# A new hand-written order for a one-core block-sorted attention and feed-forward kernel

## The chip, the cores and the metric

The kernel runs on one core of a Trainium2 chip. A core has five engines that run side by side, each through its own list of instructions: TensorE (PE in the profile; PEld is its weight load), VectorE (DVE), ScalarE (ACT), GpSimd (POOL) and SyncE (SP). They meet through semaphores: an instruction waits until a count is reached, and everything behind it on the same engine waits with it. Transfers between the chip's memory and the core's are issued by GpSimd or SyncE and then run on 16 DMA engines by themselves.

The metric is the device time of one execution in microseconds, the median of several runs. Less is better.

## The reference

Four batches of eight heads, 768 positions, head size 64. A matrix `sort_net` of 8x8 for each head is made doubly stochastic in five rounds (Sinkhorn), and mixes the eight blocks of 96 positions of k and of v. Attention is then local: each block of q sees its mixed block alone. A feed-forward layer with a leaky slope follows.

```python
for _ in range(5):
    P = P - np.max(P, axis=-1, keepdims=True)
    P = np.exp(P)
    P = P / (np.sum(P, axis=-1, keepdims=True) + 1e-09)
    P = P / (np.sum(P, axis=-2, keepdims=True) + 1e-09)
k_sorted = np.einsum('bhij,bhjcd->bhicd', P, k_b).reshape(B, H, S, D)
v_sorted = np.einsum('bhij,bhjcd->bhicd', P, v_b).reshape(B, H, S, D)
...
scores = scale * np.matmul(q_b, k_sb.transpose(0, 1, 2, 4, 3))
attn = softmax(scores)
attn_out = np.matmul(attn, v_sb).reshape(B, H, S, D)
...
x = attn_out.transpose(0, 2, 1, 3).reshape(B * S, H * D)   # 3072 x 512
h = x @ w_in                                               # 512 x 2048
g = np.maximum(h, 0.0) + alpha * np.minimum(h, 0.0)
return g @ w_out                                           # 2048 x 512
```

## The kernel before

The program first records some 1,230 operations with what each reads and writes, and then lays them out on the engines in an order that is written down by hand in two tables.

The work. A unit of attention is a group `g` of 0 to 31: one block of 96 positions of one batch, all eight heads. Groups 0 to 7 are batch 0, and so on. The steps, with the lines that the profile names:

- *Loads.* GpSimd issues the loads: q of batch 0 (L397, into a part of `hT` that is free then), k and v of batch 0 (L419, into `KS0` and `VST0`), k and v of batch 1 (L419 and L435, into `KS1` and `VST1`), `w_in` in four pieces (L907), `w_out` in two (L912), q of batches 1 to 3 in eight pieces each (L401, into `QN`). Later batches reuse the two buffers. In `QN`, `VDz`, `KSz` and `Esb` zeros are written once by GpSimd's memsets (L461, L456, L453, L474); a q piece may come only behind the memset of its own part of `QN`.
- *Sinkhorn.* Five rounds of six small VectorE operations and an exponential on ScalarE (L521); the last writes `Pb`. TensorE spreads it (L539), and VectorE makes the mixing matrix `BDK` of batch 0 (L543). For later batches L557, L560 and L565 to L585 make `BDM` and `BDV`.
- *Queries* of batch 0: six groups of 16 matmuls turn them (L600), ScalarE copies them to `QTz` (L372, the line of every plain copy on ScalarE or VectorE). Of later batches, SyncE turns them by six DMA transposes per batch (L409).
- *Keys* (`prep_k`): six groups per batch. Batch 0 multiplies `KS` by `BDK` (L600). Later batches are first copied into the zero-padded `KSz` (L616, three slots), then multiplied by `BDM` (L629). A copy of each group goes to `KT`. For batch 0 the first two groups are also copied to a pad (L642).
- *Values* (`prep_v`): eight groups per batch: a copy into place (batch 0: L653 into `hT`, later: L658 into `VDz`, four slots), matmuls (L674 or L669), a copy to `VS`.
- *Attention.* Scores (L715 for batch 0, L712 later), a row maximum on VectorE (L721), for batch 0 the scores transposed with the maximum subtracted (L736, L727) and one exponential (L759); later eight exponentials (L748) and a DMA transpose (L753). Then the product with the values (L768), a reciprocal and a scaling (L776, L779, to `xq`), and a transpose into `xT`: matmuls (L794) and a copy for batches 0 and 1, a DMA (L787) later.
- *Feed-forward.* Chunks of tokens: groups 0 and 1, 2 and 3, and from then on four groups at a time. The first layer: for each of 16 slices of `w_in` four matmuls (L823; 192 columns in the first two chunks, 384 later) into one of two banks of `psH` (in the first chunk also a bank of `psYP`), a negated relu on ScalarE (L833, into `t`) and one combining operation on VectorE (L836, into `hT`). The bank is free when L836 has run. The second layer: for each of 24 tiles of 128 tokens four times four matmuls (L862), a copy to `outstg` and a store (L876).
- *Fillers.* L808 are matmuls whose results nobody reads; they only keep TensorE busy.

What sets the order. `SEQ` lists the recorded operations by number; `arrange` walks it and appends each operation to the list of its engine. Operations that more than one engine can do carry a letter (p GpSimd, a ScalarE, d VectorE): the copies of L372, L616, L642, L653 and L658 are such. `WARM` adds fillers: `89:10:y` puts ten in front of operation 89, in bank y. `emit` works out which waits are needed. So the tables decide which engine does a copy and in which order each engine runs, and nothing else. GpSimd's operations other than DMAs run strictly one behind the other.

```python
def arrange(self, table):
    letters = {"p": "pool", "a": "act", "d": "dve"}
    ...
    for n, x in enumerate(table):
        op = self.ops[int(x.rstrip("pad"))]
        e = letters.get(x[-1], op.engs[0])
        assert e in op.engs and op.deps <= done
        done.add(op.idx)
        op.eng, op.pos, op.start = e, len(self.order[e]), float(n)
        self.order[e].append(op)
```

Of the kernel before, what the change touches and what calls it, by code (L numbers as in the profile page):

```python
# [37 lines left out]
12p 61 62 63 132 64 65 31 89 66 32 83 37 13 81 67 84 87 68 91 69 88 85 70 71 10 72 130 73 40 74 90 133 75 76 86 41  # L38
77 131 78 82 79 134 92 80 93 102 26 94d 147 103a 148 104 95 105a 100 98 99a 38 109d 106p 108p 107p 114 35 36 96a
97p 146 110p 250p 248p 113p 30 135 249p 254p 24 144 143 145 253p 20 111d 16 112d 21 141 140 142 313p 347p 139 403  # L40
404 34 33 115d 101a 158 118 116 119a 120 149 124 159 121d 125a 160 136 117d 122 137 150 123d 161 126 128 151 127a
152 129d 17 247d 162 163 164 153 177 154 155 165 166d 156 184 167 157a 196 193 194 197 185 168 169 195 27 198 170
186 187 199 202 205 188 214 203 204 200 201 220 217 215 218 206 207 189 221 219 226 222 227 229 216 190 228 230 223
224 171 231 225 208 273 235 236 237 191 238 192a 232 261 251 209 262 233 252a 239 240 241 210 263 211 255 270 212
256a 234 213d 301d 175 264 291 242 259 271 260a 265 274 267 292 272 243 266 244 279 293 282 245 280 268 281 285 294
286 258p 257p 352p 311p 300p 312p 310p 351p 348p 305p 275 338 269 174 304d 283 246d 302 303a 287 284 295 314 288
339 306 340 315 289 307a 296 316 290 176 297 320 317 276 341 318 321 319 322 178 179 298 379 308 299a 380 309a 323
342 326 349 324 327 350a 381 343 344 325 328 345 353 329 332 382 330 333 346d 354d 383 357 331 335 334 277a 361 373
336 362 358a 384 385 337 363 419 386 364 367 365 368 572p 374 402 360p 574p 391p 355p 359d 420 421 366 388 370 371
356d 387d 389d 369 372 375 392 435 436 429 393a 430 396 376 432 397d 431 377d 573p 395p 577p 390p 398 394p 445p  # L50
578p 446p 447p 449p 437 180 183 182 422 181 438 453 454 433 399d 448p 455 405 465 400 401a 459 434 466 460 461 456
451 452d 406 483 423 477 457 458 462 467 495 407 408 415 475p 413 418 411 412 479p 480p 450d 172 478a 481 506p 509p
414 463 484 424 476d 425 505p 510p 482a 496 464 409d 485 486 487 426 549 427d 488 439 507 497 492 440 508d 441 489
493 511 442 525 494 490 516 491 443a 512a 517 468 378 498 278 526 518 513 514 527 417 535p 571p 416 536p 537 469
550 515 470 471 538d 519 520 522 472 561 523 473a 539 540a 521 562 524 543 544 563 499 541 551 500 501 546 502 542d
575 503a 547 528 428 534 474 564 444 597 545 576d 555 529 606 556 548 558 607a 559 552 530 557 531 560 610 579 553a
570 613d 598 637d 612p 609p 608p 611a 582 580 583 599 581 532 635 591 636d 638p 584 585 586 587 592 639 588 626
533a 640a 589 627 590 614 615 628 641 565 593 617 618 600 566 616 642d 567 620 621 594 677 568 619 623 622 678 595a
569a 624 659 660 601 602 603 625 646 644 643 645 718p 713p 714p 661 662 663 679 604 668 704 671 629 504 410 605a
669 672 705 664 665 630 719 673 670 631 632 674 686 706 633 666a 675 692 739 554 680 752p 687 634a 648 649 748p 650  # L60
720a 676 681 689 716d 688 698 715p 647 749d 717d 658 652 690 691 699 700 173 750 693 778p 753p 854p 777p 751a 701
702 721 694 695 754 722 740 682 703 723 741 724 727 755d 683 696a 725 726 728 707 667 596 742 779 733 768 730 731
780a 729 756 708 734 783 735 757 848d 769 770 732 709 782d 758 762 759 784d 710 763 760 764 761 743 781d 744 812p
654 655 657 813p 651 849p 656 847p 850p 853p 653 814 736 803 785 737d 815a 786 765 766 804 788 789 805 767 787 745
771 711 684 806 697 738 746 794 797 838 816 798 817a 795 839 799 840 772 790 773 796 774 818 791 820 792a 775 793
841 800 801 821 807 819d 851 826 873 802 822 823 852a 824 832 881 833 827 828 874 888p 882a 834 855 885 911p 887p
875 825 808 884d 809 883d 835 856 857 842 829 912p 886a 909 861 836 830a 837 862 858 901 867 910a 843 863 889 859
860 890 902 913 864 865 903 868 869 891 895 844 914d 866 896 897 747 846 685 712 831 876 811 915 892 870 877 904
810 776 917 893 916a 935 894 871a 918 898 920 921 899 936 937 919 900 878 929 926 879 961 927 930 962 928 931 905
906 907 922 981 923 932 963 880 938 845 943 987 933 934 924d 944 964 908 982 939 946 988 989 990 983 949 947 945  # L70
940 955 941 965 950 1007 956 948 958 959 951 952 1008 1009 960 972 957 973 966 967 969 984 1033 974 970 953a 971
978 985a 979 975 976 1034 980 991 992 977 1035 1010 872 925 1036 942 968 954 1018 998 1019 995 1020 999 996 1000
1004 1059 997 1005 993 1060 1001 1002 1021 1047 1011 1061 1003 1006 1015 1016 1024 1025 1017 1012 1026 1048 1022d
1013 1085 1027 1030 1079 1080 1028 1031 1032 1029 1044 1045 1086 1041 1042 1023 1014 994 1062 986 1087 1081 1049
1046 1043 1053 1054 1055 1037 1056 1050 1067 1105 1057 1058 1070 1051d 1038 1116 1117 1068 1071 1039 1072 1069 1076
1077 1106 1078 1073 1063 1082 1074 1075 1064 1096 1083a 1097 1065 1098 1093 1094 1095 1118 1119 1120d 1107 1102
1103 1104 1040 1088 1108 1099 1089 1137 1122 1100 1101 1123 1090 1091 1124 1113 1161 1109 1128 1114 1115 1129 1110
1111 1130 1084 1066 1052 1092 1112 1125 1138 1134 1126 1127 1135 1136 1131 1139 1146 1132 1133 1147 1148 1143 1144
1145 1162 1140 1149 1163 1152 1141a 1150 1151 1155 1182 1183 1153 1154 1156 1157 1167 1168 1169 1158 1221 1184 1173
1159 1160 1174 1175 1170 1209 1179 1171 1172 1180 1181 1176 1222 1185 1191 1177 1178 1188 1189 1192 1190 1203 1210  # L80
1194 1164 1211 1121 1195 1196 1200 1186a 1187 1142 1193 1201 1165d 1202 1197 1198 1199 1204 1205 1206 1207a 1166
1208 1212 1223 1213a 1214 1224 1215 1216 1225 1226 1217 1218 1219 1220
# [947 lines left out]
```

## Time and profile before

| | us |
|---|---|
| median of 3 runs | 239.45 |
| the runs | 238.71, 241.29, 239.45 |
| the profiled execution | 238.55 |
| its span, first to last instruction | 236.8 |
| first L823 (feed-forward) starts | 30.30 |
| last L862 ends | 234.2 |

The span is what the rows of the profile divide up; the profiled execution's own time is 1.75 us longer. Mean granted clock of TensorE over the span: 0.992.

In the rows below a group of instructions reads: line, engine, operation, out<-in, sizes, count; for groups by line then busy us and mean ns of one, and the engine's idle time in front of them with what ended it. In the timeline a row starts with start and length in us, and a bracket gives the idle time in front of the instruction and its releaser.

### The profile page before, as it was taken

The page shows a single profiled execution, that of the slowest core. Times are in us where ns is not written, and L with a number is a line of the kernel's source. Part 1 is how long each engine was busy: PE and PEld are TensorE (multiplying, and loading weights), DVE is VectorE, ACT ScalarE, POOL GpSimd, SP SyncE. Part 2 cuts the span into 40 slices and gives each one's busy share as a digit, 9 for nine tenths or more (in the row PEclk, how much of TensorE's full clock was granted, in tenths as well). Part 3 has the DMA queues.
Part 4 walks back from the last instruction along what each step waited for, and adds up shares of the span by engine and source line. Part 5 has one row for each costly group of instructions (what it writes and reads, how often), then busy time and mean ns, then how long its engine had stood idle before and what let it go on. Part 6 is the DMA issues. An engine that isn't in the chain of part 4 may idle for free.

```text
span 236.8 us, 6180 instructions
## 1 busy us (share of the span) xinstructions
PE 226.7 (96%) x2474; PEld 142.7 (60%) x2503; DVE 169.4 (72%) x353; ACT 151.7 (64%) x423; POOL 73.3 (31%) x140
## 2 busy tenths in 40 slices
PE   7798899999999999999999999999999999999995
PEld 3346688687666666566655665655555555555544
DVE  4737688989899997869897667676766577644240
ACT  4465257587887988886768786756863646353232
POOL 7939824805879221148390020000000000000000
PEclk9999799999999999999999999999999999999999
DMA  5999999999999998999999797652442323400033
GB/s 95 214 214 212 205 219 195 173 212 162 181 92 145 141 168 125 154 182 194 130 100 92 210 157 157 98 95 42 125 106 69 97 50 84 132 3 0 1 136 133
DMA packets 70941, 31.36 MB, mean 132 GB/s; under 512 B 64504, under 2 KB 65280, under 8 KB 70912
## 3 DMA queue, kind: packets, MB, share of 16 engines
q0 software_dynamic: 22384, 13.63, 42.0%
q1 hardware_dynamic: 48528, 17.33, 36.9%
q8 instruction: 20, 0.33, 0.6%
q14 instruction: 9, 0.07, 0.1%
HBM read 27.28 MB, written 6.29 MB: 142 GB/s over the span
## 4 chain that ended last, share of the span: by engine, by line
PE 88%; DMA 5%; POOL 3%; DVE 2%; issue 1%; ACT 1%; POOLq 0%
PE psH L823 34%; PE psYP L862 30%; DMA VST<-in_v_dram 5%; PE psS L862 4%; PE psS L712 4%; PE psO L768 3%; PE psYP L669 2%; PE psYP L629 2%; PE psS L727 2%; PE psO L794 1%; PE psS L736 1%; PE psS L715 1%; POOL VDz L456 1%; POOL hT L653 1%; PE psH L808 1%
## 5 line engine op out<-in xcount | busy, mean ns | idle before, releaser
L836 DVE SCALAR_TENSOR_TENSOR hT<-t,omaT,psH 128x384 bf16<-128x384 f32 (+1 forms) x139 | 77.2, 571 | 36.3 <-ACT t L833 35.5
L823 PE MATMUL psH<-xT,w_in_bf 128*128 128x384 bf16 (+1 forms) x556 | 97.1, 311 | 0.0
L833 ACT ACTIVATE t<-psH 128x384 f32<-128x384 f32 (+1 forms) x139 | 62.9, 460 | 50.0 <-PE psH L823 47.7
L862 PE MATMUL psYP<-w_out_bf,hT 128*128 128x512 bf16 x308 | 77.6, 379 | 1.5
L823 PEld LDWEIGHTS psH<-xT,w_in_bf 128*128 128x128 bf16 x556 | 49.4, 98 | 29.4 <-DVE hT L836 2.1
L862 PEld LDWEIGHTS psYP<-w_out_bf,hT 128*128 128x128 bf16 x336 | 30.9, 98 | 28.2
L748 ACT ACTIVATE Esb<-psS,nf 96x96 bf16<-96x96 f32 x192 | 46.1, 345 | 2.0 <-DVE nf L721 2.0
L721 DVE TENSOR_REDUCE nf<-psS 96x8 f32<-96x768 f32 x24 | 22.8, 950 | 6.4 <-PE psS L712 6.0
L658 POOL COPY VDz<-VST 64x192 f32<-64x192 f32 x39 | 20.4, 523 | 19.2 <-DMA VST<-in_v_dram 13.5
L616 POOL COPY KSz<-KS 64x256 f32<-64x256 f32 x28 | 11.3, 404 | 33.6 <-PE psYP L629 21.2
L779 DVE TENSOR_TENSOR xq<-psO,rec 96x512 bf16<-96x512 f32 x31 | 21.2, 683 | 0.5
L401 POOL DMA_DIRECT2D QN<-in_q_dram x24 | 20.0, 838 | 2.3 <-DMA QTz<-QN 1.5
L712 PEld LDWEIGHTS psS<-KT,QTz 128*96 128x96 bf16 x192 | 12.1, 125 | 3.3
L768 PEld LDWEIGHTS psO<-VS,ET 112*128 112x128 bf16 x248 | 11.3, 99 | 3.9 <-ACT ET L759 0.5
L372 ACT ACTIVATE VS<-psYP 112x512 bf16<-112x512 f32 x15 | 10.3, 685 | 4.7 <-PE psYP L674 2.4
L768 PE MATMUL psO<-VS,ET 112*128 112x65 bf16 x248 | 13.0, 196 | 0.0
L712 PE MATMUL psS<-KT,QTz 128*96 128x96 bf16 x192 | 12.6, 208 | 0.0
L808 PE MATMUL psYP<-identb 128*128 128x512 bf16 x32 | 10.4, 460 | 0.5 <-ACT identb L372 0.5
L372 ACT ACTIVATE KT<-psYP 128x512 bf16<-128x512 f32 x15 | 8.9, 596 | 2.6 <-PE psYP L629 1.6
L372 ACT ACTIVATE outstg<-psYP 128x512 f32<-128x512 f32 x13 | 7.7, 604 | 3.2 <-PE psYP L862 3.2
L669 PEld LDWEIGHTS psYP<-BDV,VDz 128*128 128x128 bf16 x192 | 8.2, 98 | 2.4 <-ACT VS L372 0.2
L669 PE MATMUL psYP<-BDV,VDz 128*128 128x64 bf16 x192 | 9.5, 193 | 0.0
(137 smaller groups left out, 199.5 us busy)
## 6 DMA issues: line engine op xcount, KB each, us to landing
out_dram<-outstg SPq DMA_DIRECT2D x23, 256.0 KB, 2.4
KS<-in_k_dram POOLq DMA_DIRECT2D x3, 768.0 KB, 13.2
QN<-in_q_dram POOLq DMA_DIRECT2D x24, 96.0 KB, 4.7
w_in_bf<-in_moe_w_in_dram POOLq DMA_DIRECT2D x4, 512.0 KB, 16.0
w_out_bf<-in_moe_w_out_dram POOLq DMA_DIRECT2D x2, 1024.0 KB, 22.5
VST<-in_v_dram POOLq DMA_DIRECT2D x4, 384.0 KB, 17.2
hT<-in_q_dram POOLq DMA_DIRECT2D x1, 768.0 KB, 7.6
VST<-in_v_dram POOLq DMA_DIRECT2D x1, 768.0 KB, 11.5
```

Source lines behind the costliest of these rows:

```text
L372: return e.activation(o, i, ACTF.Copy) if e is nc.scalar else e.tensor_copy(o, i)
L658: G.add(SHIFT, lambda e, o2=o2, i2=i2: e.tensor_copy(o2, i2), {"dve": 424, "pool": 525}, r=vst, w=[("VDz", u % VSL, th)], prio=prio)
L669: inst = e.matmul(AP(t, off + dd * 64, [[row, 128], [1, 64]]), AP(VDz, (u % VSL * 4 + dd // 2) * 256 + dd % 2, [[VSL * 1024, 128], [2, 128]]),
L712: inst = e.matmul(o, AP(QTz[n], hp * 3072 + h4 * 768 + i * 96, [[6144, 128], [1, 96]]), AP(KT[n], (h4 * 8 + i) * bk, [[ld, 128], [64, 2], ...
L721: G.add(DVE, lambda e: e.tensor_reduce(AP(nx, 0, [[8, 96], [4, 2], [1, 4]]), AP(psX, 0, [[1024, 96], [512, 2], [96, 4], [1, 96]]), AxisLis ...
L748: inst = e.activation(AP(Esb[me], p * 128, [[1024, 96], [64, 2], [1, 48]]), AP(psX, (p // 4) * 512 + (p % 4) * 96, [[1024, 96], [48, 2], [ ...
L768: inst = e.matmul(AP(psZ, hp * 512 + h4 * 68, [[1024, 128], [1, 65]]), AP(ET[me] if far else ET[m], pos(h4, hp) * 96, [[800, nk], [1, 128] ...
L779: G.add(DVE, lambda e: e.tensor_tensor(out=AP(xq[me], 0, [[512, 96], [256, 2], [64, 4], [1, 64]]), in0=AP(psZ, 0, [[1024, 96], [512, 2], [ ...
L823: inst = e.matmul(AP(pt, poff, [[1024, 128], [1, n]]), AP(w_in_bf, kt * DFF + ft // 2 * 256 + ft % 2, [[KT_TILES * DFF, 128], [2, 128]]), ...
L833: G.add(ACT, lambda e: e.activation(AP(t1[tb], 0, [[384, 128], [1, n]]), AP(pt, poff, [[1024, 128], [1, n]]), ACTF.Relu, scale=-1.0), t_ac ...
L836: G.add(DVE, lambda e: e.scalar_tensor_tensor(out=AP(hT, ft * RING + tok % RING, [[FT_TILES * RING, 128], [1, n]]), in0=AP(t1[tb], 0, [[38 ...
L862: inst = e.matmul(AP(bank[0], bank[1], [[1024, 128], [1, n]]), AP(hT, ft * RING + tok % RING, [[FT_TILES * RING, 128], [1, 128]]), AP(w_ou ...
```

## The change

The two tables are replaced; no function, buffer, size or instruction kind changes. The diff, cut to a few rows, since its numbers say little:

```diff
 WARM = """
-89:10:y 79:7:y 93:2:y 104:2:y 114:7:y 158:2:y 153:2:h 205:1:y 207:1:y
+87:10:y 79:11:y 95:2:y 104:3:y 118:1:y 158:4:y 116:2:y 122:1:y 126:2:y 153:2:h 193:1:y 273:2:y 251:1:p
 """

 SEQ = """
-0 7 11 2 3 1 4 8 22 9 42 28 14 43 44 45 46 19 47 18 5 48 49 50 15 51 39 52 53 6 54 55 56 25 57 138 58 29 59 23 60
+0 2 11 3 7 4 8 1 9 5 10 16 40 6 132 130 13 133 87 85 131 26 138 134 147 148 24 83 91 89 81 42 43 44 45 46 47 48 49
...
 """.split()
```

Three places show what that does. The rows are instructions as they stand on an engine: line, operation, out<-in, size of the output, count.

The first place is the head of GpSimd's list, where the loads are issued (`KS0`, `VST0`: k and v of batch 0; `KS1`: k of batch 1):

```order
 L443 AFFINE_SELECT identf<-identf 128x128
-L461 MEMSET QN 128x6x32
-L456 MEMSET VDz 128x1024
-L461 MEMSET QN 128x6x32
 L419 DMA KS0<-in_k_dram 128x3072
-L456 MEMSET VDz 128x1024
 L419 DMA VST0<-in_v_dram 128x3072
+L907 DMA w_in_bf<-in_moe_w_in_dram 128x2048 x2
+L453 MEMSET KSz 128x1536
+L907 DMA w_in_bf<-in_moe_w_in_dram 128x2048 x2
 L461 MEMSET QN 128x6x32
 L419 DMA KS1<-in_k_dram 128x3072
```

The loads of k and v move in front of the memsets, and all four pieces of `w_in` in front of batch 1's k.

The second place is ScalarE's list around the last two exponentials of Sinkhorn (L521); `QTz0` are the query copies. Before:

```order
L521 ACTIVATE P32<-P32 32x64
L372 ACTIVATE QTz0<-psH 128x64x8
L372 ACTIVATE QTz0<-psO 128x64x8
L521 ACTIVATE P32<-P32 32x64
L372 ACTIVATE sel0<-identf 32x8x8x2
L372 ACTIVATE QTz0<-psS 128x64x8
```

and now:

```order
L521 ACTIVATE P32<-P32 32x64
L372 ACTIVATE QTz0<-psH 128x64x8
L372 ACTIVATE QTz0<-psO 128x64x8
L521 ACTIVATE P32<-P32 32x64
L471 ACTIVATE mkh<-mk1 128x16
```

The two copies in front of the last exponential look alike, but the first now reads the query group that TensorE turns last of the six, where before it was the second of the six.

The third place is VectorE's and TensorE's lists from the arrival of batch 0's values (the first L653) to the scores of groups 1 and 0 (L715) and their row maxima (L721). VectorE before:

```order
L372 CAST KT0<-psH 128x32x2x8
L653 COPY hT<-VST0 128x48x4
L482 TENSOR_REDUCE mkhV<-identf 128x8
L653 COPY hT<-VST0 128x48x4
L459 MEMSET ET0 128x16
L653 COPY hT<-VST0 128x48x4
L479 TENSOR_REDUCE mkjV<-identf 128x8
L476 TENSOR_REDUCE mkj<-identf 128x8
L372 CAST VS0<-psO 112x64x8
L721 TENSOR_REDUCE nm1<-psH 96x8
L372 CAST VS0<-psO 112x64x8 x2
```

and now:

```order
L642 COPY KT0<-KT0 128x32x8
L653 COPY hT<-VST0 128x48x4 x2
L464 MEMSET VS1 112x64
L653 COPY hT<-VST0 128x48x4 x2
L372 CAST KT0<-psH 128x32x2x8
L507 TENSOR_REDUCE mkhM<-mkh 128x8
L653 COPY hT<-VST0 128x48x4
L372 CAST KT0<-psO 128x32x2x8
L721 TENSOR_REDUCE nm1<-psH 96x8
L482 TENSOR_REDUCE mkhV<-identf 128x8
L721 TENSOR_REDUCE nm0<-psS 96x8
```

VectorE takes over the pad copy L642, two more value copies and key casts, and the two row maxima now stand close together, with the value casts (`VS0`) behind them. TensorE in the same stretch, before:

```order
L674 MATMUL psO<-BDK,hT 64x64 x16
L808 MATMUL psYP<-identb 128x512 x2
L715 MATMUL psH<-KT,QTz 96x96 x8
L674 MATMUL psYP<-BDK,hT 64x64 x16
L674 MATMUL psO<-BDK,hT 64x64 x32
L715 MATMUL psS<-KT,QTz 96x96 x8
L674 MATMUL psYP<-BDK,hT 64x64 x16
```

and now:

```order
L674 MATMUL psYP<-BDK,hT 64x64 x16
L808 MATMUL psYP<-identb 128x512 x4
L715 MATMUL psH<-KT,QTz 96x96 x8
L808 MATMUL psYP<-identb 128x512 x2
L674 MATMUL psO<-BDK,hT 64x64 x32
L715 MATMUL psS<-KT,QTz 96x96 x8
L674 MATMUL psYP<-BDK,hT 64x64 x16
```

Fillers stand on both sides of the first scores, and one value group less comes between the two score groups.

Over the whole program VectorE gets eleven key casts where it had five, fourteen value casts where it had sixteen, five value copies of batch 0 where it had three, and one more each of L642, the copies to `outstg` and `xT`, and the copies of L616 and L658; ScalarE and GpSimd have as many fewer (of the value casts, ScalarE has two more).

More of the change, by code (lines that the diff above doesn't have):

```diff
@@ L80 @@
-1159 1160 1174 1175 1170 1209 1179 1171 1172 1180 1181 1176 1222 1185 1191 1177 1178 1188 1189 1192 1190 1203 1210
-1194 1164 1211 1121 1195 1196 1200 1186a 1187 1142 1193 1201 1165d 1202 1197 1198 1199 1204 1205 1206 1207a 1166
-1208 1212 1223 1213a 1214 1224 1215 1216 1225 1226 1217 1218 1219 1220
+0 2 11 3 7 4 8 1 9 5 10 16 40 6 132 130 13 133 87 85 131 26 138 134 147 148 24 83 91 89 81 42 43 44 45 46 47 48 49
+50 51 52 53 54 55 56 57 58 12p 23 22 113p 15 30 14 110p 37 59 60 61 62 63 64 34 38 65 82 86 66 67 68 69 70 71 72 73
@@ L83 @@
+1163 1140 1149 1152 1141d 1164 1182 1150 1153 1151 1154 1158 1159 1160 1155 1203 1221 1170 1156 1157 1165d 1171
+1172 1167 1209 1176 1168 1169 1177 1178 1173 1222 1183 1188 1174 1175 1179 1189 1180 1181 1190 1204 1210 1191 1194
+1211 1184 1192 1193 1195 1196 1200 1201 1202 1197 1198 1199 1205 1185 1206 1223 1224 1142 1166 1084 1186a 1187
+1207d 1208 1225 1226 1212 1213a 1214 1215 1216 1217 1218 1219 1220
 """.split()
```

82 lines of the change are left out of this document (40 added, 42 removed).

## The prediction

> **What bounds the kernel now.** I read the page first: its first line, the busy shares and the granted clock in 40 slices of 5.9 us.
>
> ```profile
> span 236.8 us, 6180 instructions
> PE 226.7 (96%) x2474; PEld 142.7 (60%) x2503; DVE 169.4 (72%) x353; ACT 151.7 (64%) x423; POOL 73.3 (31%) x140
> PEclk9999799999999999999999999999999999999999
> ```
>
> TensorE is busy 96% of the span, but the share is an average, so I next read busy times by stretch (columns: length, busy us and count of PE, weight loads, VectorE, ScalarE, GpSimd; granted clock; DMA share; GB/s), and the chain in order of time (start, us, what).
>
> ```profile
> 17.00:20.00 3.00, 1.61 (x30) 0.75 (x28) 2.05 (x8) 1.18 (x3) 2.62 (x5) 1.00 1.03 210
> 23.00:24.90 1.90, 0.99 (x48) 0.80 (x42) 1.55 (x3) 1.07 (x2) 1.54 (x4) 0.98 1.08 218
> 24.90:28.10 3.20, 3.20 (x44) 2.45 (x39) 1.79 (x5) 0.81 (x1) 3.04 (x5) 0.50 1.04 209
> 30.30:40.00 9.70, 9.62 (x146) 7.92 (x143) 8.64 (x23) 5.90 (x17) 2.01 (x5) 1.00 1.17 206
> 40.00:70.00 30.00, 29.73 (x424) 22.51 (x428) 26.95 (x62) 23.35 (x65) 17.97 (x35) 1.00 1.23 169
> 70.00:90.00 20.00, 19.78 (x239) 13.23 (x241) 19.20 (x36) 17.02 (x50) 9.87 (x18) 1.00 1.14 150
> 90.00:234.20 144.20, 143.12 (x1113) 83.70 (x1130) 96.61 (x171) 91.02 (x265) 19.70 (x36) 1.00 0.61 107
> ```
>
> ```profile
> 5.45 11.47 DMA VST<-in_v_dram
> ...
> 32.67 0.21 PE psYP L808
> ...
> 36.05 0.66 PE psH L823 x8
> ...
> 39.15 0.23 PE psYP L629 x8
> ...
> 45.84 0.86 PE psYP L862 x4
> ...
> 234.17 0.38 ACT outstg L372
> ```
>
> Two regimes. From the first feed-forward matmul (30.3) to the last (234.2) PE is idle 0.08 + 0.27 + 0.22 + 1.08 = 1.65 us of 203.9. Its work there does not depend on the order, except for filler matmuls of 0.21 us. So the second regime can give back 1.65 us and two fillers, 0.4 us, at most. Anything more must come from the front: how early L823 first runs, with PE idle 1.39 us in 17 to 20 and 0.91 us in 23 to 24.9, and at half clock for 3.2 us after that.
>
> **The front, part by part.** These rows of the timeline carry its steps.
>
> ```profile
> 2.46 0.26 POOL L461 MEMSET QN<- 128x192 f32 x1
> 3.98 0.58 POOL L419 DMA_DIRECT2D KS<-in_k_dram  x1
> 8.92 0.44 PE L600 MATMUL psS<-identb,hT 64*64 64x64 bf16 x16 [1.68 <-DMA hT<-in_q_dram]
> 10.16 0.60 ACT L372 ACTIVATE QTz<-psO 128x512 bf16<-128x512 f32 x1
> 10.55 1.69 PE L808 MATMUL psYP<-identb 128*128 128x512 bf16 x7
> 10.65 0.24 ACT L521 ACTIVATE P<-P 32x64 f32<-32x64 f32 x1
> 12.83 0.29 DVE L543 TENSOR_TENSOR BDK<-mkh,psYP 128x128 bf16<-128x128 f32 x1 [0.47 <-PE psYP L539]
> 13.74 0.69 DVE L372 CAST KT<-psH 128x512 bf16<-128x512 f32 x1 [0.62 <-PE psH L600]
> 17.32 0.72 DVE L653 COPY hT<-VST 128x192 f32<-128x192 f32 x2
> 19.68 0.38 PE L715 MATMUL psH<-KT,QTz 64*96 64x96 bf16 x8 [0.98 <-POOL KT L642]
> 20.99 1.29 DVE L372 CAST VS<-psO 112x512 bf16<-112x512 f32 x2
> 23.00 0.94 DVE L721 TENSOR_REDUCE nm<-psS 96x8 bf16<-96x768 f32 x1
> 26.60 0.81 ACT L759 ACTIVATE ET<-psS 112x768 bf16<-112x768 f32 x1 [2.15 <-PE psS L727]
> ```
>
> *Loads.* Before, three memsets (from 2.46 on) stand ahead of the batch-0 k load; now it takes their place, 1.5 us earlier (3.98 to 2.46). The transfers run at 206 to 218 GB/s in the stretches above up to 40, one load behind the other, so what follows can come at most 1.5 us earlier; since q's load was already moving in that time (it lands at 8.9), I take less than half, 0.6 for v: 16.9 (5.45 + 11.47) to 16.3. Bounds: 0 and -1.5. The batch-1 k load goes behind all of w_in. The landing rows:
>
> ```profile
> L907 POOL DMA_DIRECT2D w_in_bf<-in_moe_w_in_dram x2: 538/543/548, 10.4 to 10.9; - x2
> DMA to landing us min/median/max: 16.9/17.9/18.9
> 6.17 0.55 POOL L419 DMA_DIRECT2D KS<-in_k_dram  x1
> DMA to landing us min/median/max: 13.8/13.8/13.8
> 30.30 0.83 PE L823 MATMUL psH<-xT,w_in_bf 128*128 128x192 bf16 x8
> L401 POOL DMA_DIRECT2D QN<-in_q_dram x24 | 20.0, 838 | 2.3 <-DMA QTz<-QN 1.5 <-POOL QN L461 0.6 <-issue 0.2
> L616 POOL COPY KSz<-KS 64x256 f32<-64x256 f32 x28 | 11.3, 404 | 33.6 <-PE psYP L629 21.2 <-PE psH L823 7.4 <-DMA KS<-in_k_dram 3.8
> ```
>
> w_in's last quarter lands at 10.9 + 18.9 = 29.8, half a us ahead of L823 at 30.3: nobody waits for it now, but a front shortened by over 0.5 us would. Moved ahead of k's 3.1 to 3.7 us of transfer, it lands near 26, so by itself this edit is worth nothing; it lets the rest count. Its price is at batch 1's keys: k moves from 20.0 to about 29.5, and GpSimd's first KSz copy waits for it with eight q loads and the second half of w_out queued behind. Their data are far back in a full DMA queue, so that costs nothing while the queue stays full. GpSimd then needs w_out's issue, six q issues (0.84 us each), three memsets like that at 2.46 and four KSz copies (0.40) before the first prep_k of batch 1, some 9 us: about 38.5. PE wanted it 8.9 us behind L823 (39.15 less 30.3); with two L823 groups fewer in between, and a score group and a filler more, I count 9.3, so 38.7. Bounds 0 and +0.7; I take 0.
>
> *Sinkhorn.* The last exponential (10.65) now stands behind two query copies, the first of which reads the sixth and last query group: 8.92 + 1.63 (where the filler starts) = 10.55, plus two copies at 0.5: 11.6, so BDK moves from 12.83 to about 13.9. Cover: the values land only at 16.3 to 16.9. Four key casts instead of one are now VectorE's; two stand before the values (0.69 each, ending near 16), two behind.
>
> *Values to first scores.* Behind the landing VectorE now has five value copies (0.36) and two key casts (0.69): 3.2 us, from 16.5 to 19.8, where the first score (19.68, held up by GpSimd's L642) was before. L642 is now VectorE's, ahead of the landing. No gain here.
>
> *Scores to FFN.* The second row maximum (23.00) stood behind two casts of 0.65 and the alpha row; now it follows the first maximum and a small reduction: near 22.0, so 1.0 earlier. Three of the five VectorE casts stay, ScalarE takes five of eight (0.69) in place of three; the exponential at 26.60 comes to about 25.9. From there the old chain to L823 took 3.7 us, much of it at half clock. PE gets nine fillers (4, 2, 1, 2) between the value groups where two stood: 1.9 us against 0.4, in a stretch that had 2.3 us idle. I take it that the clock holds; the chain, limited by ScalarE and VectorE, then takes 3.5. L823 at 29.4: **-0.9**. Bounds: +0.5 (clock halves as before, sinkhorn's delay uncovered) and -1.7 (the above plus v a full 0.8 earlier).
>
> **Behind the first L823.** Fillers: three (2 and 1) instead of two, **+0.2**. VectorE gets six key casts more and two VS casts fewer (net 2.8 us at 0.69), two value copies more (0.7), and one each of L642 and the output, xT, KSz and VDz copies, none longer than a cast: 0 to 3.4, I take 2.1. Of these 5.6 us, three key casts, two value copies and L642 less two VS casts, 1.8, lie ahead of L823; 3.8 lie behind. ScalarE loses six key casts and gains two VS casts. VectorE was busy 89% from 30 to 70 and 96% from 70 to 90 (19.20 of 20.00). Bounds: 0 and, if all falls in the tight stretch with 0.8 to spare, +3.0. Because the order of the engines was shifted to match, I take **+0.3**, near the low end.
>
> Sum: 236.8 - 0.9 + 0.2 + 0.3 = 236.4. The profiled run took 238.55, 1.75 over its span, and the median of the three others, 239.45, is 0.9 above that. I put the typical run halfway: 236.4 + 1.75 + 0.45 = **238.6 us**.
>
> **The rivals.** *Given back at batch 1's queries (no change).*
>
> ```profile
> L409 SPq DMA_TRANSPOSE QTz<-QN x1: 1325/1325/1325, 49.5 to 49.5; - x1
> DMA to landing us min/median/max: 5.9/5.9/5.9
> DMA to landing us min/median/max: 4.0/4.0/4.0
> 56.87 0.52 PE L712 MATMUL psS<-KT,QTz 128*96 128x96 bf16 x8
> ```
>
> SyncE turns batch 1's queries from 49.5; the first lands at 55.4 and PE uses it at 56.9. The new order has 0.75 us less PE work between L823 and that L712 (four L862 matmuls, 0.86, and four L823, 0.33, fewer; a filler, 0.21, and eight L669, about the 0.23 of L629, more), so PE arrives at 29.4 + 25.8 = 55.2. If the last q load, now issued near 43.7 instead of 39.8, or batch 2's loads, now issued near 47 instead of 41, hold the turn where it was or 0.7 us later, PE waits 0.3 to 0.9 us and the front's gain is gone: 238.9 to 239.5, say 239.2. For it: 5.9 us here with loads in flight, 4.0 (third row, the turn at 82.3) without. Against: the queue ahead is the same bytes and starts earlier. The Trainium skill (DMA: Bandwidth & Descriptors, section Queues, rings and completion order) says that an engine takes turns between the queues packet by packet; 5.9 against 4.0 agrees, and by that rule later loads stretch the turns.
>
> *VectorE becomes the bound (slower).* Place: 30 to 90. Price: the 3.0 us above instead of 0.3: 241.3, up to 242.1 if nothing is spare. It decides once over 0.8 us of added casts falls between 70 and 90, or over 3 us before it. Against: ScalarE's relief shortens the copies that VectorE waits for.
>
> *The whole front (faster).* The clock holds, v is 0.8 early and the idle of the second regime halves: 236.8 - 1.7 - 0.8 + 0.2 = 234.5, and with the same 2.2 around it 236.7. The Trainium skill (TensorE: Matmul & The Clock Gate, Part 1) has the clock halved only after a whole idle window of about 3.4 us. The trace disagrees: the longest gap ahead of the fall at 24.9 was 0.98 us. By that rule no gap of the new order would cost clock and the sum stays 236.4; by the fall that the trace shows, up to half of 3.2 us could be paid again.
>
> **Numbers.** Forecast 0.48, given back 0.25, VectorE 0.15, whole front 0.12. About 1%, 2.4 us, is what a measurement of this kernel tells from no change. Faster by more (below 237.05): most of the last case and a little of the first, 0.14. Slower by more (above 241.85): half of VectorE's and a remainder for disturbed runs, 0.11. Range 236.7 to 241.3 leaves out about half of the last case and half of VectorE's; the forecast's own is 237.6 to 239.6.
>
> **What would show it.** Right: L823 first near 29.4, clock at 1.00 from 20 to 30, w_in landed before 27, PE idle under 2.2 us behind L823. Wrong: a PE wait on prep_k near 38, on L712 near 55, or VectorE over 97% from 70 to 90 with PE gaps on L836; a first L823 after 30.3 with half clock would show that the front's steps were misjudged.

## The result and the profile after

| | before | after |
|---|---|---|
| median of 12 runs, us | 240.16 | 244.59 |
| lowest and highest, us | 238.36, 241.73 | 241.86, 260.03 |
| ratio after to before | | 1.0133, 95% interval 1.0097 to 1.017 |
| the profiled execution, us | 238.55 | 243.7 |
| its span, us | 236.8 | 242.0 |
| first L823 starts, us | 30.30 | 29.90 |
| last L862 ends, us | 234.2 | 239.3 |

The change made the kernel 1.3% slower; the forecast was 238.6 us, no change. Five runs of the changed kernel, and the profiled executions of the later kernels `k_late`, `loads_early` and `fillers`, were disturbed: the ratios leave such runs out (the medians are then 240.16 and 242.76), and of those three profiles only the times of transfers are read below, unless the text says so.

The head of the page after, and the granted clock in 40 slices of 6 us:

```profile
span 242.0 us, 6183 instructions
PE 229.0 (95%) x2481; PEld 143.5 (59%) x2511; DVE 174.5 (72%) x364; ACT 148.6 (61%) x417; POOL 70.7 (29%) x135
PEclk9999999998899999999999999999999999999999
```

The dip of the clock has moved. Before it stood in the slices from 24 to 30 us; now it stands in the two from 54 to 66. The busy times by stretch, with the columns of the prediction, tell the rest:

```profile
17.00:20.00 3.00, 1.46 (x21) 0.65 (x20) 2.97 (x7) 1.98 (x4) 2.76 (x5) 1.00 1.08 217
23.00:24.90 1.90, 1.90 (x46) 1.16 (x46) 1.18 (x2) 0.87 (x2) 0.00 (x0) 1.00 1.08 218
24.90:28.10 3.20, 3.14 (x69) 2.18 (x68) 2.00 (x7) 1.98 (x3) 0.00 (x0) 1.00 1.04 214
30.30:40.00 9.70, 9.44 (x141) 7.39 (x140) 8.07 (x22) 5.41 (x16) 8.85 (x17) 1.00 1.17 207
40.00:70.00 30.00, 27.16 (x380) 21.40 (x380) 23.93 (x55) 21.45 (x59) 13.60 (x28) 0.94 1.14 149
70.00:90.00 20.00, 19.65 (x225) 12.79 (x226) 16.95 (x33) 17.71 (x55) 13.00 (x22) 1.00 1.07 119
90.00:239.40 149.40, 147.47 (x1172) 86.78 (x1190) 104.07 (x188) 90.24 (x264) 21.37 (x40) 1.00 0.62 111
```

From 30.3 us on TensorE is idle 0.26 + 2.84 + 0.35 + 1.93 = 5.4 us, where it was 1.65 us before: 3.7 us more. In the stretch from 40 to 70 the clock is 0.94, which is 6% of 30 us, 1.8 us of work. Against that stands a first L823 0.4 us earlier. Together 5.1 us, which is what the last L862 is late by. So the clock held in the front, and what was lost was lost behind it, most of it between 40 and 70 (2.6 us of the idle time and the 1.8 us).

Where? The view of TensorE's waits (what waited and for whom: us in total, times, longest), then TensorE's timeline there:

```profile
PE psS L712 <- DMA QTz<-QN: 2.6, 1, 2.6
```

```profile
55.70 0.41 PE L768 MATMUL psO<-VS,ET 112*128 112x65 bf16 x8
58.73 0.88 PE L712 MATMUL psS<-KT,QTz 128*96 128x96 bf16 x8 [2.62 <-DMA QTz<-QN]
59.41 1.48 PE L823 MATMUL psH<-xT,w_in_bf 128*128 128x192 bf16 x8
60.68 1.74 PE L862 MATMUL psYP<-w_out_bf,hT 128*128 128x512 bf16 x4
62.26 0.49 PE L823 MATMUL psH<-xT,w_in_bf 128*128 128x192 bf16 x4
```

TensorE reaches batch 1's first scores at 56.1, 0.8 us earlier than before, and stands for 2.6 us because SyncE's first turn of batch 1's queries has not landed. Then eight L823 take 1.48 us (0.83 at 57.4 before): the clock reads 0.50 to 62.1, and the half clock that was paid for at 25 us before is paid for here.

The turn itself was issued no later than before. The rows of its line, and of the load of batch 2's k, with their times from issue to landing:

```profile
L409 SPq DMA_TRANSPOSE QTz<-QN x1: 1521/1521/1521, 49.0 to 49.0; - x1
...
DMA to landing us min/median/max: 9.7/9.7/9.7
```

```profile
L419 POOL DMA_DIRECT2D KS<-in_k_dram x1: 584/584/584, 48.7 to 48.7; - x1
...
DMA to landing us min/median/max: 9.0/9.0/9.0
```

The turn starts at 49.0 (49.5 before) and takes 9.7 us instead of 5.9. What is new beside it is the load, issued at 48.7 instead of 41.2. GpSimd's timeline shows why: before, the two loads of batch 2 stood right behind the first value copies,

```profile
38.87 1.09 POOL L658 COPY VDz<-VST 64x192 f32<-64x192 f32 x2 [7.63 <-DMA VST<-in_v_dram]
39.83 0.82 POOL L401 DMA_DIRECT2D QN<-in_q_dram  x1
40.64 0.56 POOL L435 DMA_DIRECT2D VST<-in_v_dram  x1
41.17 0.61 POOL L419 DMA_DIRECT2D KS<-in_k_dram  x1
```

and now behind two query loads and a dozen copies of keys and values:

```profile
30.35 0.39 POOL L616 COPY KSz<-KS 64x256 f32<-64x256 f32 x1 [9.61 <-DMA KS<-in_k_dram]
...
43.99 0.82 POOL L401 DMA_DIRECT2D QN<-in_q_dram  x1
...
47.75 0.54 POOL L435 DMA_DIRECT2D VST<-in_v_dram  x1
48.34 0.52 POOL L658 COPY VDz<-VST 64x192 f32<-64x192 f32 x1
48.71 0.58 POOL L419 DMA_DIRECT2D KS<-in_k_dram  x1
```

In both kernels the turn starts when the last query piece has landed, at 49.0 and 49.5. But GpSimd's loads no longer follow each other without a gap. The stretch from 46 to 50, before and then after (the last number is GB/s):

```profile
46.00:50.00 4.00, 4.00 (x68) 3.27 (x67) 3.28 (x8) 2.76 (x7) 1.01 (x3) 1.00 1.64 200
```

```profile
46.00:50.00 4.00, 3.95 (x70) 3.42 (x70) 3.87 (x11) 3.14 (x8) 3.06 (x7) 1.00 1.28 103
```

### The profile page after: what moved, and what is told of

It is laid out like the page before. It is cut to its first block, busy times and chain, and to the rows that moved or that the text cites. A ratio compares the mean times of both kernels' runs of the same rounds, so it can differ in the third digit from the quotient of the medians.

```text
span 242.0 us, 6183 instructions
## 1 busy us (share of the span) xinstructions
PE 229.0 (95%) x2481; PEld 143.5 (59%) x2511; DVE 174.5 (72%) x364; ACT 148.6 (61%) x417; POOL 70.7 (29%) x135
## 3 DMA queue, kind: packets, MB, share of 16 engines
q0 software_dynamic: 22384, 13.63, 41.2%
## 4 chain that ended last, share of the span: by engine, by line
PE 68%; DMA 20%; POOL 8%; issue 2%; ACT 1%; DVE 0%; POOLq 0%
PE psH L823 29%; PE psYP L862 26%; DMA KS<-in_k_dram 10%; DMA QTz<-QN 4%; DMA ET<-Esb 4%; PE psS L862 4%; PE psS L712 3%; POOL QN L401 2%; PE psO L768 2%; DMA QN<-in_q_dram 2%; PE psYP L669 2%; PE psYP L629 1%; POOL KSz L616 1%; POOL VDz L658 1%; POOL w_in_bf L907 1%
## 5 line engine op out<-in xcount | busy, mean ns | idle before, releaser
L823 PE MATMUL psH<-xT,w_in_bf 128*128 128x384 bf16 (+1 forms) x556 | 99.1, 312 | 0.4 <-DVE rec L776 0.4
L862 PE MATMUL psYP<-w_out_bf,hT 128*128 128x512 bf16 x308 | 79.6, 382 | 1.5
L823 PEld LDWEIGHTS psH<-xT,w_in_bf 128*128 128x128 bf16 x556 | 50.3, 99 | 29.8 <-DVE rec L776 0.7
L862 PEld LDWEIGHTS psYP<-w_out_bf,hT 128*128 128x128 bf16 x336 | 31.5, 98 | 29.3 <-issue 0.6
L658 POOL COPY VDz<-VST 64x192 f32<-64x192 f32 x38 | 20.0, 526 | 29.1 <-PE psYP L669 13.5
L721 DVE TENSOR_REDUCE nf<-psS 96x8 f32<-96x768 f32 x24 | 22.7, 945 | 5.6 <-PE psS L712 5.1
L401 POOL DMA_DIRECT2D QN<-in_q_dram x24 | 19.9, 839 | 0.3 <-POOL QN L461 0.3
L616 POOL COPY KSz<-KS 64x256 f32<-64x256 f32 x27 | 10.8, 400 | 28.7 <-PE psYP L629 13.9
L712 PE MATMUL psS<-KT,QTz 128*96 128x96 bf16 x192 | 13.0, 211 | 2.6 <-DMA QTz<-QN 2.6
L712 PEld LDWEIGHTS psS<-KT,QTz 128*96 128x96 bf16 x192 | 12.0, 127 | 5.2 <-DMA QTz<-QN 2.7
L808 PE MATMUL psYP<-identb 128*128 128x512 bf16 x40 | 12.8, 444 | 0.7 <-ACT identb L372 0.7
L372 ACT ACTIVATE VS<-psYP 112x512 bf16<-112x512 f32 x14 | 9.6, 688 | 0.6 <-PE psYP L669 0.3
L669 PEld LDWEIGHTS psYP<-BDV,VDz 128*128 128x128 bf16 x192 | 8.4, 98 | 2.7
L862 PE MATMUL psS<-w_out_bf,hT 128*128 128x512 bf16 (+1 forms) x46 | 9.5, 342 | 0.1
L669 PE MATMUL psYP<-BDV,VDz 128*128 128x64 bf16 x192 | 9.5, 193 | 0.0
```

Source lines behind the costliest of these rows:

```text
L401: G.add(POOL, lambda e, h=h: e.dma_start(AP(QN, h * 128 + (h // 4) * 64, [[6144, 128], [1024, 6], [1, 64]]), AP(q.tensor, b * HB + h * S * ...
L658: G.add(SHIFT, lambda e, o2=o2, i2=i2: e.tensor_copy(o2, i2), {"dve": 424, "pool": 525}, r=vst, w=[("VDz", u % VSL, th)], prio=prio)
L669: inst = e.matmul(AP(t, off + dd * 64, [[row, 128], [1, 64]]), AP(VDz, (u % VSL * 4 + dd // 2) * 256 + dd % 2, [[VSL * 1024, 128], [2, 128]]),
L712: inst = e.matmul(o, AP(QTz[n], hp * 3072 + h4 * 768 + i * 96, [[6144, 128], [1, 96]]), AP(KT[n], (h4 * 8 + i) * bk, [[ld, 128], [64, 2], ...
L721: G.add(DVE, lambda e: e.tensor_reduce(AP(nx, 0, [[8, 96], [4, 2], [1, 4]]), AP(psX, 0, [[1024, 96], [512, 2], [96, 4], [1, 96]]), AxisLis ...
L823: inst = e.matmul(AP(pt, poff, [[1024, 128], [1, n]]), AP(w_in_bf, kt * DFF + ft // 2 * 256 + ft % 2, [[KT_TILES * DFF, 128], [2, 128]]), ...
```

## The experiments

The theories. A: batch 2's loads, issued late, are still moving beside the turn and stretch it. B: the turn is slow for another reason. And two causes for the lateness: GpSimd's 9.6 us wait for batch 1's k, which the chain of waits after names (k of batch 1, issued at 7.0, takes 23.22 us of it), or merely the place of the loads in GpSimd's list.

**1. k back in front.** `k_first`, GpSimd's list:

```diff
+L419 DMA KS1<-in_k_dram
 L907 DMA w_in_bf<-in_moe_w_in_dram x2
 L453 MEMSET KSz
 L907 DMA w_in_bf<-in_moe_w_in_dram x2
 L461 MEMSET QN
-L419 DMA KS1<-in_k_dram
 L912 DMA w_out_bf<-in_moe_w_out_dram
```

> The changed kernel, with batch 1's k load back in front of w_in's four pieces, and nothing else moved. k lands near 18 instead of 30.2, w_in's last piece near 30.0 instead of 26.6. Theory A with GpSimd's wait for k as the cause of the late loads: GpSimd no longer stands from 20.7 to 30.35, but is held by the copies of batch 1's values until v lands (39.2), so the last query loads and batch 2's loads are issued only 1 to 2 us earlier; the turn lands near 57, the wait at L712 falls from 2.6 to about 1 us and the half clock behind it gets shorter: a span of 239.5 to 241, less 0 to 0.3 for L823 if it waits for w_in. Rival C (where k lands has no part in it): wait and span as now, 2.6 and 242.

Measured: ratio 1.0159 (1.009 to 1.0229), no better than the change as a whole. k landed at 19.9 and GpSimd's long wait was gone, but the loads came only 0.3 us earlier:

```profile
38.66 1.08 POOL L658 COPY VDz<-VST 64x192 f32<-64x192 f32 x2 [7.07 <-DMA VST<-in_v_dram]
...
43.24 0.40 POOL L616 COPY KSz<-KS 64x256 f32<-64x256 f32 x1 [1.67 <-PE psYP L629]
...
47.45 0.54 POOL L435 DMA_DIRECT2D VST<-in_v_dram  x1
...
48.40 0.58 POOL L419 DMA_DIRECT2D KS<-in_k_dram  x1
```

GpSimd now waits for v instead of k, and then for TensorE (L629) to free a slot of `KSz`. The wait at L712 was 2.2 us. So the expectation of about 1 us was wrong, and the part of the change that looks boldest in the diff, k behind `w_in`, costs nothing that these four runs can show. The chain had named it truly as what released GpSimd, but behind it stood another wait of the same end.

**2. The query loads ahead.** `issues_first` keeps k behind `w_in`, and issues all eight query loads and the second half of `w_out` in front of the first `KSz` copy:

```diff
-L616 COPY KSz<-KS1
 L401 DMA QN<-in_q_dram
 L912 DMA w_out_bf<-in_moe_w_out_dram
-L401 DMA QN<-in_q_dram x4
+L401 DMA QN<-in_q_dram x7
+L616 COPY KSz<-KS1 x2
...
 L658 COPY VDz<-VST1 x2
-L401 DMA QN<-in_q_dram
 L658 COPY VDz<-VST1 x2
 L616 COPY KSz<-KS1
-L401 DMA QN<-in_q_dram
```

> The changed kernel, k still behind w_in, but all eight query loads and the second half of w_out are issued in front of GpSimd's first copy of batch 1's keys, which waits for k. The transfers are one behind the other, so the last query piece still lands at 48.5 to 49.5; batch 2's loads are issued near 45 instead of 47.75 and 48.71. Theory A: the turn lands at 56 to 57.5, the wait at L712 is 0 to 1.4 us and the span 237.5 to 240.5. Rival B (only the queries' landing counts): turn and span as now, 58.7 and 242.

Measured: ratio 1.0103 (1.0057 to 1.015), not to be told from the change's 1.0133; span 240.1. The loads of batch 2 came at 47.2 and 48.2, 0.5 us earlier, not near 45. The turn, issued at 49.3, landed at 57.9, and because the front was 0.9 us later in this execution, TensorE waited 0.9 us only; the clock stayed at 1.00 behind it. The queries were all issued by 30.2, and the turn still took 8.6 us: its own loads are not the cause.

**3. Batch 2's loads away from the turn.** `loads_late`:

```diff
-L435 DMA VST0<-in_v_dram
 L658 COPY VDz<-VST1
-L419 DMA KS0<-in_k_dram
 L658 COPY VDz<-VST1 x6
+L435 DMA VST0<-in_v_dram
+L419 DMA KS0<-in_k_dram
 L435 DMA VST0<-in_v_dram
```

> The changed kernel, with batch 2's half v load and k load (issued at 47.75 and 48.71 us) moved on GpSimd behind the copies of batch 1's values, so that they are issued near 57. Theory A (these loads, still moving when SyncE turns batch 1's first queries, stretch the turn): the first turn is issued near 49.0 as now and lands at 53 to 54 instead of 58.7, TensorE reaches the first L712 near 56.1 and does not wait, the clock stays at 1.00 from 56 to 66, and the 2.6 us of wait and some 1.8 us of half clock go: a span of 237.5 to 238.0, about level with the kernel before. Rival B (the turn is slow by itself or is held by the queries' own loads): it still takes over 8 us and the span stays near 242.

Measured: ratio 1.0294 (1.0244 to 1.0344), slower still. Yet the first half of the expectation came out exactly. The turn took 4.1 us and TensorE did not wait at L712, but the loads now came too late for batch 2's values:

```profile
L409 SPq DMA_TRANSPOSE QTz<-QN x1: 1325/1325/1325, 49.4 to 49.4; - x1
...
DMA to landing us min/median/max: 4.1/4.1/4.1
```

```profile
PE psYP L669 <- POOL VDz L658: 3.9, 1, 3.9
```

The wait had moved from L712 to L669, and the half clock (0.83 from 70 to 80) with it. The time alone would have spoken against theory A; the two waits speak for it.

**4. The k load alone, behind one more copy.** `k_late` moves only k's load past the next L658, to 52.4.

> The changed kernel, with only batch 2's k load (768 KB, issued at 48.71) moved on GpSimd behind the next copy of batch 1's values, so that it is issued near 52.2; the half v load at 47.75 and the other half at 57.5 stay, so that the copies of batch 2's values are not late, as they were when all three loads went together near 59. Theory A (the turn lands when the load issued ahead of it is through, at 4.15 us where none is): the first turn lands at 53.2 to 54.5, TensorE does not wait at the first L712 (arrival 56.1 to 57), the clock stays at 1.00 and the span is 237.5 to 239. Rival D (any load in these microseconds stretches the turn as much): the turn still lands after 57, and the span stays at 241 to 242.

Measured: ratio 1.0038 (1.0005 to 1.0071), against 1.0133 (1.0097 to 1.017) for the change. The first turn landed at 53.6, 4.8 us after its issue and 1.1 us after the half v load beside it (52.45). With none beside it the turn takes 4.1 us, so rival D is out: a load of half the size costs it 0.7 us. The third turn, which now met k's load, landed only at 67.7.

**5. The loads early.** `loads_early` issues the last query load and both loads of batch 2 behind the first two value copies (k at 43.0), with three key copies behind them:

```diff
 L658 COPY VDz<-VST1 x2
-L401 DMA QN<-in_q_dram
-L658 COPY VDz<-VST1 x2
+L401 DMA QN<-in_q_dram x2
+L435 DMA VST0<-in_v_dram
+L419 DMA KS0<-in_k_dram
+L616 COPY KSz<-KS1 x3
+L658 COPY VDz<-VST1 x3
...
```

> The changed kernel, with the last query load and batch 2's half v and k loads issued together behind the seventh query load near 42 to 44 us, about where the kernel before issues them (39.8 to 41.2), and three key copies in front of the value copies behind them. Theory A: the loads flow without a gap behind the queries, k lands near 54.5 instead of 57.7 and the first turn near 55.5 instead of 58.7; TensorE, there at 56 to 57, does not wait; span 237.5 to 239. Against it: the copies on GpSimd are up to 1.9 us later, which may cost a wait on KSz or VDz at 46 to 52. Rival E (the cause is that the queue ran thin, whatever is behind it, or the order of TensorE): the wait of 2 us or more stays.

Measured: ratio 1.0039 (1.0012 to 1.0067), again clear of the change's. k landed at 55.35 and the turn at 56.4. TensorE came to L712 at 60.8 only in that profile, so that it did not wait there says nothing on rival E.

**6. All loads ahead of all copies.** `all_ahead` is `issues_first` with batch 2's two loads behind the eighth query load, at 30.4 for k.

> The changed kernel, k still behind w_in, with all eight query loads, the second half of w_out and batch 2's half v and k loads issued one behind the other from 20.7 us on, in front of GpSimd's first copy of batch 1's keys. No load that the first turn meets then waits for a copy that waits for TensorE. Theory A: the transfers are one gapless row, the last query piece lands near 49.3, k near 54.5, the first turn near 55.5; TensorE gets to the first L712 at 56.5 to 57.3 and does not wait; span 238.2 to 239.2 against 240.1 with the queries alone moved ahead (issues_first), and the runs lie closer together than those of the changed kernel (241.9 to 260). Rival E (the wait is tied to the order of TensorE): a wait of 1 us or more stays, span 240 or more.

Measured: ratio 1.0014 (0.9985 to 1.0042), level with the kernel before. The runs that the ratio uses lie between 240.13 and 242.18, those of the change between 241.86 and 245.48. Against `issues_first`, GpSimd's list differs by the place of these two loads alone, the other engines' lists not at all, and the intervals do not overlap: this is the cleanest price of their lateness, about 0.9% or 2 us. k landed at 55.0, the turn at 55.9, as expected, and TensorE did not wait at L712. The span, 240.5, was longer than expected, because in this execution the first L823 came at 31.8 and other waits were left (below).

**7. The loads late in the kernel before.** `before_loads_late` moves batch 2's two loads in the old order, k from 41.2 to 47.0.

> The kernel before, with only batch 2's half v load and k load moved on GpSimd, from 40.6 and 41.2 us to behind the key copies that end near 47. Theory A: the first turn of batch 1's queries lands at 57.5 to 59 instead of 55.5, TensorE waits 0.6 to 2 us at the first L712 (56.9 now), and with half clock behind it the span is 1 to 4 us longer, 238 to 241. Rival B: the lateness of the two loads does not matter, the turn lands within 0.5 us of 55.5 and the span stays at 236.8 to 237.3.

Measured: ratio 1.0012 (0.9982 to 1.0043): nothing, although the turn landed at 58.2 as theory A has it. TensorE came to L712 at 58.7 only. Its clock had been 0.50 from 24.9 to 30.3 and the first L823 had come at 32.1. The late turn was hidden behind a late front, in this execution; of the other nine only the times are known.

The first turn and batch 2's k load in the fourteen profiled executions say the same. Times in us:

| kernel | k issued | k lands | turn issued | turn lands | turn behind k |
|---|---|---|---|---|---|
| before | 41.2 | 54.41 | 49.51 | 55.46 | 1.05 |
| after | 48.7 | 57.73 | 49.03 | 58.69 | 0.96 |
| `k_first` | 48.4 | 57.59 | 48.65 | 58.57 | 0.98 |
| `issues_first` | 48.2 | 56.84 | 49.26 | 57.86 | 1.02 |
| `before_loads_late` | 47.0 | 57.45 | 48.95 | 58.19 | 0.74 |
| `loads_early` | 43.0 | 55.35 | 49.80 | 56.41 | 1.06 |
| `all_ahead` | 30.4 | 54.96 | 49.91 | 55.90 | 0.94 |
| `all_ahead_front` | 31.0 | 54.53 | 49.80 | 55.55 | 1.02 |
| `before_fill_late` | 47.5 | 57.19 | 49.08 | 57.88 | 0.69 |
| `before_fillers` | 41.0 | 54.18 | 48.64 | 57.29 | 3.11 |
| `k_late`, `late_and_front` | 52.4, 52.1 | later | 48.72, 49.34 | 53.55, 53.58 | |
| `loads_late` | 59.0 | later | 49.39 | 53.54 | |
| `fillers` | 51.1 | later | 49.42 | 56.10 | |

In nine of the ten executions in which k's load was ahead of the turn, the turn landed 0.7 to 1.1 us after it, whenever that was; the tenth, at 3.1, has no explanation here.

Why the turn ends right behind the load can be read from the DMA queues (queue, packets, MB, share of 16 engines). GpSimd's loads run in the software queue, SyncE's turns in the hardware queue. The changed kernel from 53 to 56, with both at work, then the kernel before from 54 to 56, with the load through:

```profile
q0 software_dynamic: 80, 0.49, 93.3%
q1 hardware_dynamic: 75, 0.02, 4.7%
```

```profile
q1 hardware_dynamic: 1957, 0.48, 116.9%
q0 software_dynamic: 4, 0.00, 0.1%
```

Side by side, each queue gets about as many packets as the other. But a packet of the load holds some 6 KB, one of the turn under 0.5 KB, so the turn hardly moves until the load is through, and then moves quickly.

**8. A shorter front on top.** `late_and_front` is `k_late` with GpSimd's two value copies in front of its memsets of `VDz`, and VectorE's last two key casts ahead of two value copies:

```diff
-L653 COPY hT<-VST0
+L653 COPY hT<-VST0 x3
 L456 MEMSET VDz
 L474 MEMSET Esb
 L456 MEMSET VDz
-L653 COPY hT<-VST0 x2
```

> As the run before the last but one (batch 2's k load issued near 52.2), and at the front GpSimd copies its other two values of batch 0 in front of its two 1 us memsets of VDz instead of behind them, and VectorE makes its last two key casts ahead of two value copies. In the runs so far the first L823 starts 13.9 to 14.05 us after batch 0's v lands (13.4 in the kernel before, 16.1 where the clock was halved), and TensorE waits 0.7 to 1.6 us there for a key cast and 0.9 for a value copy. Expected: first scores (L715) 2.5 us after v's landing instead of 3.1 to 4.2, first L823 12.8 to 13.3 us after it, and with the turn landing by 54.5 no wait at L712, so that the span is 236.3 to 238, 0.7 to 1.2 below the kernel with the late load alone. Rival: what the front gains is given back by half clock or at L712, and the span is the same as with the late load alone.

Measured: the first L823 came 13.1 us after v's landing instead of 13.9 to 14.05, as expected. And the ratio was 1.016 (1.0085 to 1.0235), worse than `k_late`: TensorE came 0.3 us earlier to the first L712 and waited 1.8 us at the third, for a turn that landed at 67.2 beside k (62.7) and v (67.3), and 0.9 us for `VDz`. The profile of `k_late` shows the same two waits (2.0 and 0.9 us), so they do not explain the difference between the two kernels; that stays open. `all_ahead_front` has the same front and the loads of `all_ahead`:

> As the run before it, and GpSimd's two value copies ahead of its memsets and VectorE's last two key casts ahead of two value copies, which in late_and_front brought the first L823 from 14.0 to 13.1 us behind v's landing. Theory A: TensorE is 0.8 us earlier at the first L712 (55.7 to 56.5), the turn lands near 55.5 as before, and at most 0.3 us is waited there: span 0.5 to 0.9 below all_ahead, 237.4 to 238.6; against the kernel before a ratio of 0.990 to 0.998. If the front's gain is given back further on: the same span as all_ahead.

Measured: ratio 1.0036 (1.0006 to 1.0067), in the profiled execution a span of 238.8 with the first L823 at 29.6, the clock at 1.00 throughout, and L712 at 55.63, right behind the landing. The span was 1.7 us below that of `all_ahead`, but the ratios overlap, so the gain in the front is not shown in the time. No version beat the kernel before.

What kept it from being faster can be read from its waits:

```profile
PE psO L768 <- DMA ET<-Esb: 1.0, 2, 0.6
PE psH L823 <- DVE xq L779: 0.8, 1, 0.8
```

The kernel before has no such wait at either place. One is another transpose (ET); the other names VectorE, whose `xq` had ended just before. Waits on ET (0.4 to 1.1 us) and one of L823 at 161 to 167 us (0.3 to 0.8) are in all seven profiles of the new order that are read in full. From the first L823 to the last L862 `all_ahead_front` takes 206.5 us, the kernel before 203.8. No run took these waits away, so what that would give is argued only.

**9. Fillers.** `before_fillers` adds three L808 ahead of the first L715 and four ahead of the last L674 group of the old order; `before_fill_late` moves the loads as in 7 as well.

> The kernel before with seven filler matmuls more in its front: five instead of two ahead of the first L715, and four in the 0.88 us gap ahead of the fourth L674 group at 24.6. Its clock was 0.50 from 24.9 to 28.1 in the profiled execution and to 30.3 and beyond in another, with the first L823 13.4 and 16.1 us behind v's landing. If those gaps bring the clock down: clock 0.9 to 1.00 from 24.9 to 30.3, first L823 12.5 to 13.4 us behind v, and the time 238.0 to 239.2 against a median of 240.1 (ratio 0.991 to 0.996). Rival: the clock falls anyway, 239.8 to 240.6.

> As before_fillers, and batch 2's half v and k loads behind the key copies near 47 us, as in before_loads_late, where it cost nothing: there the front was late (first L823 at 32.1), so that TensorE came to the first L712 at 58.7, 0.5 us after the turn had landed (58.2). Theory A: with the front early, TensorE comes near 56 to 57 and waits for a turn that still lands at 58 to 58.7; the gain of the fillers is given back: a time of 239.5 to 241, 1 to 2 us above before_fillers. Rival (the late loads cost nothing in this order of the engines): the same time as before_fillers.

Measured: 1.0002 (0.9973 to 1.0032) and 1.0029 (0.9994 to 1.0064). Neither answers its question. The first L823 came 15.9 and 16.2 us after v's landing, with a clock of 0.68 from 24.9 to 30.3 in the first and 1.00 in the second. So the front was not made early, and nothing could be given back. Nor is half clock alone what makes the old front late, since the second is late without it. In these two and in `before_loads_late` TensorE stands 1.5 to 2.5 us ahead of an L674 at 24.9 to 26.7, where it stood 0.88 us in the profile shown; the profile names no cause.

`fillers` adds 13 L808 in front of the changed kernel's first L712, to tell the price of the clock from that of the wait.

> The changed kernel, with 13 filler matmuls (L808, 2.8 us at 0.216 us each, results not read) on TensorE in front of the first L712, so that it works while it waits for the turn. It tells the price of the clock from that of the wait. If the half clock behind the wait costs what the trace shows (L823 at 0.186 instead of 0.083 us each from 59.4 to 62.2, about 1.8 us with L712): the clock stays at 1.00 from 56 to 66 and the span falls from 242.0 to 240.2 to 240.8. If the clock's fall is not due to the idle time, or costs nothing that is not lost anyway: 241.8 to 242.5.

Measured: ratio 1.0085 (1.0052 to 1.0118) against 1.0133 (1.0097 to 1.017). The difference, 0.5% or 1.2 us, has the expected sign and size, but the intervals overlap: not settled.

## Why the prediction was wrong

- **The failed step** is "Behind the first L823". The sum put +0.5 us there (0.2 for fillers, 0.3 for VectorE) and held no term for a wait at batch 1's queries; the time from the first L823 to the last L862 grew by 5.5 us (203.8 to 209.4). The reason for a price of 0 was that what GpSimd's wait for k holds up is "far back in a full DMA queue, so that costs nothing while the queue stays full". For the eight query loads this came out: the last landed at 49.0 (49.5 before). It did not for batch 2's loads, which stand behind them and which the sum left out. They came only when the queue had run thin: 103 GB/s from 46 to 50 where it had moved 200. So they ran beside the turn.
- **The rival that came true was mis-sized.** "Given back at batch 1's queries" had the place, the mechanism and even the time of the loads right (about 47 expected, 47.75 and 48.71 measured). It let them hold the turn "where it was or 0.7 us later", which gave a wait of 0.3 to 0.9 us. The turn was 3.2 us later and the wait 2.6. The working had two rows to bound it, 5.9 us beside loads and 4.0 without, and took the first as the worst. But in that row k's load had had an 8 us start; one that starts with the turn keeps it for the whole of its own 9.0 us. The rule of the Trainium skill named there (DMA: Bandwidth & Descriptors, section Queues, rings and completion order) is that an engine takes turns between the queues packet by packet. The trace agrees (80 and 75 packets above); the rule was cited, but not worked out with the sizes of the packets.
- **A term was missing**: half clock behind a long wait, about 1.8 us in this trace. Wait, half clock and the small waits (about 1 us) make up the 5.5 us. That the half clock costs its 1.8 us in time is read from the trace; `fillers` did not settle it.
- **The second regime's idle time**, 1.65 us, was hardly idle: the page before counts 2474 matmuls beside 2503 weight loads, so 29 matmuls are missing from it. `before_fillers`, with 2510 of each, shows 0.1 us idle from its first L823 to its last L862. Of the profile after, 30 are missing, so the 3.7 us between the two stands.
- **The front**: the clock held at 1.00 from 20 to 30, as forecast, and `w_in` landed at 26.6. L823 came at 29.90, not 29.4. v landed at 15.85 in the profile after (16.92 before), but the forecast's 0.6 us does not show: over ten executions with the new head of GpSimd's list v lands at 15.9 to 17.0, over four with the old at 16.0 to 16.9. "Values to first scores" was mis-sized: the first L715 starts 4.2 us behind v's landing (20.02, after a wait of 1.57 us for a key cast), where the working had about 3.5. Counted from v to the first L823, the new order takes 13.9 to 14.05 us in four executions and 15.3 in `all_ahead`, whose clock was at half from 10.0 to 13.4. The old takes 13.4 in the profile shown and 15.9 to 16.2 in three others (two of them with the seven fillers). So the profiled front before was the best of four, and the base was a lucky one. Its mean clock says so too: 0.992, where 58 of the 67 runs of the kernel before that stand beside the experiments have 0.985 or 0.986, which is about 1.4 us more lost to the clock.
- **Batch 1's keys**, 0: right, no wait on prep_k appears. **VectorE**, +0.3 and the rival of 241.3: it was busy 85% from 70 to 90 (16.95 of 20), not over 97%, with no wait of TensorE on it there; no cost of it shows.
- The text named the sign that decided: "a PE wait on L712 near 55".

## What to carry to other kernels

When a list is rearranged, price a load by what it will run beside at the time it is issued, not by the bytes ahead of it: a transfer that nobody waits for can hold up one that somebody does. Issue such loads ahead of copies that wait for the engine they feed, or else a late engine makes its own transfers later. And before a gain at the front is counted, find the first wait behind it whose end does not move with it; and look at more than one execution of the base.

## What the runs showed of the hardware

- The first turn of batch 1 (a DMA transpose) took 4.1 us with no load beside it and 5.8 to 9.9 us where k's load was ahead of it, and landed about 1 us behind that load in nine of ten executions. A turn issued at 52.4, beside later loads, took 14.8 us (`late_and_front`).
- The clock fell behind waits of 2.2 us (`k_first`), 2.6 (the change) and 3.9 (`loads_late`), and behind one of 0.9 us (`issues_first`) it stayed at 1.00. The length of the wait alone does not decide: it also stayed at 1.00 behind 1.57 us at 20.0 in the change, and fell at 24.8 in the kernel before with 0.91 us idle in the 3.4 us ahead. The Trainium skill (TensorE: Matmul & The Clock Gate, Part 1) has it fall after a whole idle window of about 3.4 us; here less was enough.
- Half clock came in pieces of one length: 3.4 us in the change (0.85, 0.50, 0.50, 0.50 and 0.94 in the microseconds from 58 to 63) and in the kernel before (24.8 to 28.2), twice that in `before_loads_late` (24.7 to 31.6). So a fall cost 1.7 us of work or a multiple of it, however short the wait ahead of it.
- The same list gives landings of the first loads that differ by over 1 us from one execution to the next, and a first L823 that differs by 1.8 us (30.30 and 32.09 in the old order).
